# Attention fused with two feed-forward layers: for the tiles that hold the last 64 rows of two heads, the turned weights become the fixed operand of the product with the values, and the result is turned back

## The chip, the cores and the metric

The kernel runs on one core of a Trainium2 chip. The metric is device time in microseconds (us) of one launch, as the median of three runs. A core has a matrix engine (TensorE, PE in the profile; its weight loads are listed apart as PEld), a vector engine (DVE), a scalar engine (ACT), GpSimd (POOL), and SyncE (SP), which issues the DMAs here. Each engine takes its instructions in a fixed order and waits at an instruction until what it needs is there.

A matrix multiplication has a *fixed* operand (`lhsT`, loaded into the array first, up to 128 columns) and a *moving* operand (`rhs`, streamed through it column by column). An fp32 multiplication appears in the trace as two matmul records, each with a weight load of its own.

## The reference

```python
# q, k, v: (4 batches, 8 heads, 576 rows, 64)
scores = scale * np.matmul(q, k.transpose(0, 1, 3, 2))
kth = np.partition(scores, -32, axis=-1)[..., -32:-31]
scores = np.where(scores >= kth, scores, -1e9)
attn = softmax(scores)                              # over the last axis
attn_out = np.matmul(attn, v)
x = attn_out.transpose(0, 2, 1, 3).reshape(2304, 512)
x = leaky(x @ w_in1) @ w_out1                       # 512 -> 2048 -> 512
out = act2(x @ w_in2) @ w_out2                      # 512 -> 2048 -> 512
```

All of it is float32. `softmax`, `leaky` (the larger of h and 0.01 h) and `act2` (a parabola between -1 and 1) stand here for lines of the same meaning.

## The kernel before, in words

**Attention units.** A sequence of 576 rows is four tiles of 128 rows and a rest of 64. A unit of kind "m" is two tiles (256 rows) of one head. A unit of kind "r" is one tile of 128 rows made of the last 64 rows of head 2h and the last 64 rows of head 2h+1 (`st_scores`, L706 to L710). There are 64 units "m" and 16 units "r": twelve of these stand among the units of batch 2 and four among those of batch 3 (`REMS`, L32).

A unit goes through four steps. `scores` multiplies queries and keys on PE, and ACT copies the two halves (288 columns) to `s`. `topk` finds the 32nd largest score per row with MAX8 and MATCH_REPLACE on DVE (L570, L574), and ACT, POOL and DVE make the normalized weights `e` (L583 to L611). `pt_bank` turns `e` (128 rows x 576) into blocks of 116 keys x 128 rows on PE (L624; the last block has 112 keys) and ACT copies them to `ptr`. `pv` (L634) multiplies them with the values.

**`pv` of a unit "r" before.** The fixed operand is a block of values, `vl`: 116 keys x 128 columns, the 64 columns of one head twice. The moving operand is the 64 columns of `ptr` that belong to that head. So for each of the two heads there are five multiplications (one for each block of keys) of 64 moving columns, and the result has the value index on the partitions and the rows on the columns, as the next stage wants it. `gather` then copies 64x64 of it for each head to `xr` (L739, recorded at L361). Values of the first two batches take the same fp32 path for units "m", with 256 moving columns.

**Feed-forward layers.** Rows of 256 (one "m" pair of tiles for all heads) or 512 go through two layers. `hidden` (L804) and `sums` (L842) put fp32r multiplications on PE, three for each product (L766 to L768, and L837 to L839 for the second layer's sums). The groups are listed in `FLOW`; the last group, rows (3,0), (3,1) and "r", can start only when the last units are out, and "r" is the row block that all 16 units "r" fill.

**What sets the order.** All work is recorded as operations with an engine, an estimated duration, a priority and dependences (`Plan.op`). `Plan.run` (L130) plays this through in time and takes, on each engine, the ready operation of lowest priority number; the order that results is the program. Attention has the number of its unit (0 to 79), feed-forward products 10000 and more, so they fill what attention leaves free on PE. For a unit "r" before, each of the ten products is recorded with 112 ns (L657). From unit 20 on attention has two PSUM banks (6 and 7) for all its products (L335).

Of the kernel before, what the change touches and what calls it, by code (L numbers as in the profile page):

```python
# [23 lines left out]
NEG = -3.0e38  # L24
STEEP = 1.0e33
KB = 116
BUFS = dict(x=2, xraw=2, kk=5, vl=4, vv=4, kraw=3, px=8, vraw=2, qraw=3, qh=2, s=6, wk=3, e=4, m8=3, nb=3, sums=2, rc=2,
            pt=3, ptr=3, xb=2, t=3, gr=2, gt=3, wraw=2, wa=2, wb=2)
PREP = (0.7, 4.5, 0.05, 14, 14.0, 0.25)
HOP = 180  # L30
# [223 lines left out]
def t_a(n, psum=False):  # L254
    return 0.82 * n + (50 if psum else 95)
# [10 lines left out]
def t_m(n):  # L266
    return n / 2.4 + 14
# [7 lines left out]
def kernel(  # L275
# [4 lines left out]
    km: bass.AP,  # L280
    vm: bass.AP,
    vd: bass.AP,
    w_in1: bass.AP,
    w_out1: bass.AP,
    w_in2: bass.AP,
# [4 lines left out]
    nc = tc.nc  # L290
    B, H, D2, S = km.shape
    D = D2 // 2
# [3 lines left out]
    T = 256  # L296
    XW = 512
    QM = S // 128 * 128
    REM = S - QM
    HALF = S // 2  # L300
    NJ = vm.shape[3]
    cols = [slice(j * KB, min(S, (j + 1) * KB)) for j in range(NJ)]
    rows_of = [c.stop - c.start for c in cols]
    scale = 1.0 / float(D) ** 0.5
# [76 lines left out]
    def pe(fn, ns, w, r, prio, also=()):  # L381
        P.op("PE", ns, fn, w=w, r=r, prio=prio, also=also)
# [6 lines left out]
    idt = fixed([128, 128], F32, "idt")  # L389
# [98 lines left out]
    def lean_of(b, h):  # L488

        return b * H + h < NLEAN  # L490

    def plain_of(b, h):

        return b * H + h < NPLAIN
# [24 lines left out]
    def v_whole(b, h, pr):  # L519

        vt = new("vl", [128, NJ, 2 * D])
        dma(vt, lambda: vd[b, h], 320, [vt], [], pr + 0.5)
        return vt

    def q_new(src, n, pr, plain=False):
        raw = new("qraw", [128, QM])
        dma(lambda: raw()[:, 0:n], src, n / 2, [raw], [], pr)
        if plain:
            return raw
        qh = new("qh", [128, 2, QM], F32R)  # L530
        split(lambda a: qh()[:, a, 0:n], lambda: raw()[:, 0:n], n, qh, [raw], 0, pr)
        return qh
# [81 lines left out]
    def pt_bank(es, js, lean, pr):  # L614

        ps = bank(pr)
        p = rows_of[js[0]]
        blocks = [(e, j) for j in js for e in es]
        n = 128 * len(blocks)
        raw = new("ptr", [128, 512])  # L620

        def tr():
            for i, (e, j) in enumerate(blocks):
                nc.tensor.transpose(ps()[0:p, i * 128:(i + 1) * 128], e()[:, cols[j]], idt())  # L624

        pe(tr, 109 * len(blocks), [ps], list(es) + [idt], pr, [raw])
        act(lambda: raw()[0:p, 0:n], lambda: ps()[0:p, 0:n], t_a(n, True), [raw], [ps], pr)
        if lean:
            return raw
        pt = new("pt", [128, 2, 512], F32R)  # L630
        split(lambda a: pt()[0:p, a, 0:n], lambda: raw()[0:p, 0:n], n, pt, [raw], 0, pr)
        return pt

    def pv(es, jobs, lean, pr):  # L634

        w = 128 * len(es)
        per = 512 // w
        todo = [list(range(j, min(j + per, NJ - 1))) for j in range(0, NJ - 1, per)] + [[NJ - 1]]
        banks = [(pt_bank(es, js, lean, pr), js) for js in todo]
        out_ps = bank(pr)  # L640
        for bi, (pt, js) in enumerate(banks):
            for part in range(1 if lean else 2):
                def mm(bi=bi, pt=pt, js=js, part=part):
                    for (vt, c0, c1) in jobs:
                        for jj, j in enumerate(js):
                            p = rows_of[j]
                            c = slice(jj * w + c0, jj * w + c1)
                            nc.tensor.matmul(  # L648
                                out_ps()[:, c0:c1], lhsT=vt()[0:p, j, :],
                                rhs=pt()[0:p, c] if lean else pt()[0:p, part, c],  # L650
                                start=bi == 0 and part == 0 and jj == 0 and c0 == 0,
                                stop=bi == len(banks) - 1 and (lean or part == 1),
                                skip_group_check=True,
                            )

                n = jobs[0][2] - jobs[0][1]
                ns = max(4 * n / 2.4 if lean else t_m(n), 112)  # L657
                pe(mm, ns * len(js) * len(jobs), [out_ps], [pt if lean else (pt, (0, part))] + [vt for vt, _, _ in jobs], pr)
        return out_ps

    x_raw = {"r": fixed([128, KD, T], F32, "xr", lambda: pools["xr"])}

    def get_xraw(g):
        if g not in x_raw:
            x_raw[g] = new("xraw", [128, KD, T])
        return x_raw[g]
# [24 lines left out]
    def st_scores(u, pr):  # L691
        kind, b, a, h = u
        if kind == "m":
            plain = plain_of(b, h)
            if a == 0 or b not in JOINT:
                k_cur[b, h], v_cur[b, h] = k_new(b, h, pr, plain), v_new(b, h, pr)
            kk, vt = k_cur[b, h], v_cur[b, h]
            if b not in JOINT:
                q_cur["t"] = q_new(lambda: qm[b, h][:, a * T:(a + 1) * T], T, pr, plain)
            elif a == 0:  # L700
                q_cur["t"] = q_new(lambda: qm[b, h], QM, pr, plain)
            qh = q_cur["t"]
            t0 = 2 * a if b in JOINT else 0
            return dict(u=u, tiles=[scores([(qh, t0 + t, kk)], pr, plain) for t in range(2)], jobs=[(vt, 0, T)],
                        scale=scale / 2 if plain else scale)
        ks = [k_cur[b, 2 * h + e] if b == u_batch[0] else k_new(b, 2 * h + e, pr) for e in range(2)]  # L706
        vs = [v_whole(b, 2 * h + e, pr) for e in range(2)]
        qh = q_new(lambda: qp[b, h], T, pr)
        return dict(u=u, tiles=[scores([(qh, e, ks[e]) for e in range(2)], pr)], scale=scale,
                    jobs=[(vs[e], e * REM, (e + 1) * REM) for e in range(2)])  # L710

    def second():

# [6 lines left out]

    def st_out(s, pr):
        kind, b, a, h = s["u"]
        lean = kind == "r" or lean_of(b, h)
        ps = pv(s["es"], s["jobs"], lean, pr)
        if kind == "m":
            x = get_xraw((b, a))
            if h % 2 == 0 and not lean:
                xb_cur[a] = new("xb", [128, T])
            xb = xb_cur.get(a)
            c = h // 2  # L730
            gather(ps, (h % 2) * 64, 0, T, lambda: x()[:, c], (x, (c, h % 2)), xb, lean, pr)
            if h % 2 == 1 and not lean:
                P.op("P", t_p(T), lambda: nc.gpsimd.tensor_tensor(out=x()[:, c], in0=x()[:, c], in1=xb(), op=ALU.add),
                     w=[(x, (c, 0)), (x, (c, 1))], r=[xb], prio=pr)
        else:
            x = x_raw["r"]
            c = slice(b * REM, (b + 1) * REM)
            for e in range(2):
                gather(ps, e * 64, e * REM, (e + 1) * REM, lambda: x()[:, h, c], (x, (h, b, e)), None, True, pr)  # L739
# [205 lines left out]
def laid_out(inputs):  # L945

    x = {n: np.ascontiguousarray(inputs[n]) for n in _INS}
    q, k, v = x["q"], x["k"], x["v"]
    B, H, S, D = q.shape
    QM = S // 128 * 128  # L950
    REM = S - QM
    data = []

    def twice(a):
        a = a.transpose(0, 1, 3, 2)
        return np.concatenate([a, a], axis=2)

    data.append(("qm", twice(q[:, :, :QM])))
    qp = np.zeros((B, H // 2, 2 * D, 4 * REM), q.dtype)
    last = twice(q[:, :, QM:])  # L960
    for e in range(2):
        o = e * 128 + e * REM
        qp[..., o:o + REM] = last[:, e::2]
    data.append(("qp", qp))
    data.append(("km", twice(k)))
    nj = -(-S // KB)
    vp = np.zeros((B, H, nj * KB, D), v.dtype)
    vp[:, :, :S] = v
    vm = np.zeros((B, H, 128, nj, D), v.dtype)
    vm[:, :, :KB] = vp.reshape(B, H, nj, KB, D).transpose(0, 1, 3, 2, 4)  # L970
    data.append(("vm", vm))
    data.append(("vd", np.concatenate([vm, vm], axis=4)))
    for n in _INS[3:]:
        w = x[n]
        w = w.view(np.int64) if w.dtype == np.float64 else w
        if "_in" in n:
            kd, nf = w.shape[0] // 128, w.shape[1] // 128
            w = w.reshape(kd, 128, nf // 2, 2, 128).transpose(2, 1, 3, 0, 4)
        else:
            nf = w.shape[0] // 128  # L980
            w = w.reshape(nf // 2, 2, 128, w.shape[1]).transpose(0, 2, 1, 3)
        data.append((n, w.reshape(nf // 2, 128, -1)))
    data.append(("ident", np.eye(128, dtype=np.float32)))
    return [(n, np.ascontiguousarray(a)) for n, a in data]
# [18 lines left out]
```

## Time and profile before

| what | value |
|---|---|
| three runs | 1239.53, 1240.49, 1244.61 us; median 1240.49 us |
| profiled execution, its own time | 1239.65 us |
| its span, first to last instruction | 1237.9 us |
| PE busy | 1169.7 us (94%) |
| PEld busy | 996.9 us (81%) |
| DVE, ACT, POOL busy | 891.9, 854.3, 718.6 us |
| granted clock of TensorE, mean | 0.979 of full speed |
| moved by DMA | 238.58 MB, 193 GB/s |

Busy time of PE has modelled ends, since matmuls are pipelined: a record's duration is longer than the time until the next can start. What one record costs in a dense stretch is read from the distance between starts. The 16 units "r" multiply with the values between 495 and 938 us of the span; the page shows PE at nine tenths or more in nearly all 40 slices from the tenth on, while DVE, ACT and POOL fall off after some 930 us, when attention is over and the feed-forward layers of the last rows are left.

### The profile page before, as it was taken

To read this page: it belongs to the slowest core of one execution; us is meant where nothing else is said; L and a number is where in the kernel's file an instruction comes from. 1 tells how busy PE (TensorE), PEld (TensorE's weight loads), DVE (VectorE), ACT (ScalarE), POOL (GpSimd) and SP (SyncE) were. 2 spreads that over 40 slices of the span, in tenths; PEclk is the share of its full clock that TensorE was granted. 3 is DMA by queue.
4 is the path that set the end of the run, shared out by engine and by line. 5 is a ranking of instruction groups with operands and counts; after the bars stand their busy time and mean duration, and the time that the engine had idled before them with its cause. 6 is when DMAs were issued, how large, how long until landed. Compare 5 with 4: busy or idle time off the path is not lost.

```text
span 1237.9 us, 19284 instructions
## 1 busy us (share of the span) xinstructions
PE 1169.7 (94%) x6448; PEld 996.9 (81%) x6448; DVE 891.9 (72%) x1791; ACT 854.3 (69%) x1905; POOL 718.6 (58%) x820
## 2 busy tenths in 40 slices
PE   5678988887999999999999999999999999999998
PEld 4557878776878888888888888888888888888886
DVE  7999999999999999895999988979992000012221
ACT  6777999987888889897879788888643212142222
POOL 2434888764667669696878767778654222242221
PEclk8788999999999999999999999999999999999999
DMA  9744898986567555556566564443354423433333
GB/s 322 265 164 131 310 338 306 327 339 224 190 236 245 196 183 196 199 191 212 165 213 200 194 214 140 159 147 124 131 170 153 158 106 128 137 136 136 116 107 101
DMA packets 75444, 238.58 MB, mean 193 GB/s; under 512 B 8400, under 2 KB 14672, under 8 KB 71248
## 3 DMA queue, kind: packets, MB, share of 16 engines
q1 hardware_dynamic: 75344, 237.34, 55.3%
q8 instruction: 51, 0.84, 0.3%
q14 instruction: 49, 0.40, 0.1%
HBM read 199.03 MB, written 38.27 MB: 192 GB/s over the span
## 4 chain that ended last, share of the span: by engine, by line
PE 75%; ACT 10%; DVE 8%; POOL 4%; issue 2%; DMA 1%; SPq 0%; POOLq 0%; ACTq 0%; DVEq 0%
PE bank L766 14%; PE bank L768 14%; PE bank L767 14%; PE bank L648 10%; PE bank L624 5%; PE bank L547 5%; PE bank L837 5%; PE bank L839 5%; PE bank L838 5%; DVE m L570 3%; DVE wk L574 2%; ACT e L592 2%; DVE wb L456 2%; ACT s L361 1%; ACT e L363 1%
## 5 line engine op out<-in xcount | busy, mean ns | idle before, releaser
L377 POOL TENSOR_TENSOR gt<-gr,gt 128x512 fp32r<-128x512 f32 x144 | 191.6, 1332 | 253.9 <-ACT gt L361 132.2
L570 DVE MAX8 m<-wk 128x8 f32<-128x576 f32 x432 | 309.1, 747 | 0.8
L813 DVE TENSOR_SCALAR t<-bank 128x512 f32<-128x512 f32 x72 | 49.4, 687 | 241.5 <-PE bank L768 241.0
L574 DVE MATCH_REPLACE8 wk<-m,wk 128x576 f32<-128x576 f32 x288 | 212.3, 742 | 0.0
L766 PE MATMUL bank<-x,ring 128*128 128x512 f32 (+1 forms) x576 | 211.6, 367 | 0.2 <-DVE gr L816 0.2
L768 PE MATMUL bank<-x,ring 128*128 128x512 f32 (+1 forms) x576 | 205.8, 357 | 0.0
L767 PE MATMUL bank<-x,ring 128*128 128x512 f32 (+1 forms) x576 | 205.4, 357 | 0.0
L624 PE MATMUL bank<-idt,e 128*116 128x128 f32 (+1 forms) x720 | 114.4, 287 | 27.3 <-POOL e L609 22.1
L361 ACT COPY s<-bank 128x288 f32<-128x288 f32 x288 | 108.1, 404 | 35.4 <-PE bank L547 33.7
L624 PEld LDWEIGHTS bank<-idt,e 128*116 128x116 f32 (+1 forms) x720 | 87.8, 141 | 51.0 <-POOL e L609 29.8
L648 PE MATMUL bank<-ptr,vl 116*128 116x256 f32 (+3 forms) x640 | 124.8, 348 | 3.8 <-ACT ptr L361 3.6
L570 DVE MAX8 m<-s 128x8 f32<-128x576 f32 x144 | 103.9, 746 | 31.2 <-ACT s L361 31.2
L361 ACT COPY ptr<-bank 116x512 f32<-116x512 f32 (+1 forms) x224 | 107.6, 511 | 25.6 <-PE bank L624 24.3
L768 PEld LDWEIGHTS bank<-x,ring 128*128 128x128 f32 x576 | 108.4, 188 | 17.4
L377 POOL TENSOR_TENSOR pt<-ptr,pt 116x512 fp32r<-116x512 f32 (+1 forms) x96 | 106.3, 1130 | 25.1 <-ACT pt L361 23.5
L609 POOL TENSOR_SCALAR e<-e,rc 128x576 f32<-128x576 f32 x144 | 108.3, 762 | 20.3 <-DVE rc L607 17.5
L648 PEld LDWEIGHTS bank<-ptr,vl 116*128 116x128 f32 (+1 forms) x640 | 104.0, 204 | 19.0 <-ACT ptr L361 7.6
L766 PEld LDWEIGHTS bank<-x,ring 128*128 128x128 f32 x576 | 108.9, 189 | 11.7 <-DVE gr L816 0.7
L767 PEld LDWEIGHTS bank<-x,ring 128*128 128x128 f32 x576 | 108.9, 189 | 11.5 <-POOL x L377 0.5
L363 ACT ACTIVATE t<-t,half 128x512 f32<-128x512 f32 x72 | 52.0, 723 | 92.8 <-DVE t L813 92.6
L766 PE MATMUL bank<-gt,ring 128*128 128x512 f32 (+1 forms) x320 | 114.7, 358 | 0.0
L547 PE MATMUL bank<-kk,qh 128*128 128x288 f32 x512 | 101.2, 305 | 14.2 <-ACT s L361 6.3
(85 smaller groups left out, 2797.1 us busy)
## 6 DMA issues: line engine op xcount, KB each, us to landing
ring<-scr SPq DMA_DIRECT2D x224, 512.0 KB, 3.6
scr<-px SPq DMA_DIRECT2D x64, 512.0 KB, 4.2
vl<-in_vd_dram SPq DMA_DIRECT2D x56, 320.0 KB, 3.8
wraw<-in_moe_w_in_dram SPq DMA_DIRECT2D x16, 1024.0 KB, 6.0
wraw<-in_moe_w_out_dram SPq DMA_DIRECT2D x16, 1024.0 KB, 7.4
kraw<-in_km_dram SPq DMA_DIRECT2D x56, 288.0 KB, 4.2
qraw<-in_qm_dram SPq DMA_DIRECT2D x24, 256.0 KB, 4.0
out_dram<-t SPq DMA_DIRECT2D x16, 256.0 KB, 3.4
```

The lines of the kernel that those rows point to most:

```text
L361: nc.scalar.copy(out=out_(), in_=in_())
L363: nc.scalar.activation(out=out_(), in_=in_(), func=func, **a)
L377: lambda: nc.gpsimd.tensor_tensor(out=out_(), in0=in0(), in1=in1(), op=ALU.subtract),
L547: nc.tensor.matmul(ps()[:, 0:HALF], lhsT=qh()[:, at] if plain else qh()[:, part, at], rhs=kk()[:, c * HALF:(c + 1) * HALF], start=(i == 0) ...
L570: vec(lambda i=i, c=c, src=src: nc.vector.max(out=m()[:, i, c], in_=src()), 664, [(m, (i, r))], [src], pr)
L574: vec(lambda i=i, c=c, src=src, w=ws[i]: nc.vector.match_replace(out=w(), in_to_replace=m()[:, i, c], in_values=src(), imm_value=NEG), 720 ...
L609: P.op("P", T_NORM, lambda i=i: nc.gpsimd.tensor_scalar(out=es[i](), in0=es[i](), scalar1=rc()[:, i:i + 1], scalar2=1.0, op0=ALU.mult, op1 ...
L624: nc.tensor.transpose(ps()[0:p, i * 128:(i + 1) * 128], e()[:, cols[j]], idt())
L648: nc.tensor.matmul(out_ps()[:, c0:c1], lhsT=vt()[0:p, j, :], rhs=pt()[0:p, c] if lean else pt()[0:p, part, c], start=bi == 0 and part == 0 ...
L766: nc.tensor.matmul(ps, lhsT=wh, rhs=xh, start=first, stop=False, skip_group_check=True)
L767: nc.tensor.matmul(ps, lhsT=wh, rhs=xl, start=False, stop=False, skip_group_check=True)
L768: nc.tensor.matmul(ps, lhsT=wl, rhs=xh, start=False, stop=last, skip_group_check=True)
```

## The change

For units "r" `pv` is replaced by `pv_pair`. The turned weights `ptr` (116 keys x 128 rows) are the fixed operand, and the moving operand is a block of both heads' values side by side, 116 keys x 128 columns, from a new input `vp`. Five multiplications give 128 rows x 128 value columns. ACT copies that to a new buffer `y` (one buffer, 128x128), PE turns it with the identity into the same PSUM bank, and the same two 64x64 copies to `xr` follow. One DMA of 320 KB loads `vp` where two of 320 KB loaded `vd` twice. The multiplications are recorded with 218 ns each and the turn with 109 ns. For units "m" `pv` is written more simply and does what it did.

```diff
+    def v_pair(b, h, pr):
+
+        vt = new("vl", [128, NJ, 2 * D])
+        dma(vt, lambda: vp[b, h], 320, [vt], [], pr + 0.5)
+        return vt
...
+    def pv_pair(e, vt, pr):
+
+
+        banks = pt_banks([e], True, pr)
+        ps = bank(pr)
+        y = new("y", [128, 2 * D])
+        for bi, (pt, js) in enumerate(banks):
+            def mm(bi=bi, pt=pt, js=js):
+                for jj, j in enumerate(js):
+                    p = rows_of[j]
+                    nc.tensor.matmul(
+                        ps()[:, 0:2 * D], lhsT=pt()[0:p, jj * 128:(jj + 1) * 128], rhs=vt()[0:p, j, :],
+                        start=bi == 0 and jj == 0, stop=bi == len(banks) - 1,
+                    )
+
+            pe(mm, 2 * 109 * len(js), [ps], [pt, vt], pr, [y] if bi == 0 else [])
+        act(y, lambda: ps()[:, 0:2 * D], t_a(2 * D, True), [y], [ps], pr)
+        pe(lambda: nc.tensor.transpose(ps()[:, 0:128], y(), idt()), 109, [ps], [y, idt], pr)
+        return ps
...
-        vs = [v_whole(b, 2 * h + e, pr) for e in range(2)]
+        vt = v_pair(b, h, pr)
         qh = q_new(lambda: qp[b, h], T, pr)
-        return dict(u=u, tiles=[scores([(qh, e, ks[e]) for e in range(2)], pr)], scale=scale,
-                    jobs=[(vs[e], e * REM, (e + 1) * REM) for e in range(2)])
+        return dict(u=u, tiles=[scores([(qh, e, ks[e]) for e in range(2)], pr)], scale=scale, v=vt)
...
         else:
+            ps = pv_pair(s["es"][0], s["v"], pr)
             x = x_raw["r"]
...
     data.append(("vd", np.concatenate([vm, vm], axis=4)))
+    data.append(("vp", np.concatenate([vm[:, ::2], vm[:, 1::2]], axis=4)))
```

Two places show how the order moves. On PE, around the first unit "r" (batch 2, heads 0 and 1), the kernel before has these rows; L648 is `pv`, L624 turns the next unit's weights, L766 to L768 are feed-forward products:

```order
L648 MATMUL bank6_219<-ptr0_296,vl0_150 128x64 x4
L648 MATMUL bank6_219<-ptr0_296,vl1_158 128x64 x4
L648 MATMUL bank6_219<-ptr1_301,vl0_150 128x64
L648 MATMUL bank6_219<-ptr1_301,vl1_158 128x64
L766 MATMUL bank4_211<-x1_2345,ring4_493 128x512
L767 MATMUL bank4_211<-x1_2345,ring4_493 128x512
L768 MATMUL bank4_211<-x1_2345,ring4_493 128x512
L624 MATMUL bank7_225<-idt_146,e1_244 116x128 x4
```

In the changed kernel the same place reads so; L677 is the product in `pv_pair`, L684 the turn back, L631 and L792 to L794 are the former L624 and L766 to L768:

```order
L677 MATMUL bank6_222<-vl0_153,ptr0_299 128x128 x4
L677 MATMUL bank6_222<-vl0_153,ptr1_304 128x128
L792 MATMUL bank4_214<-x1_2348,ring4_496 128x512
L793 MATMUL bank4_214<-x1_2348,ring4_496 128x512
L794 MATMUL bank4_214<-x1_2348,ring4_496 128x512
L631 MATMUL bank7_228<-idt_149,e1_247 116x128 x4
L792 MATMUL bank4_214<-x1_2348,ring4_496 128x512
L793 MATMUL bank4_214<-x1_2348,ring4_496 128x512
L794 MATMUL bank4_214<-x1_2348,ring4_496 128x512
L684 MATMUL bank6_222<-idt_149,y0_4660 128x128
```

Ten products became five, and the turn stands behind six feed-forward products and four turns of the next unit's weights. On ACT, at the same unit, the kernel before has:

```order
L361 COPY xb_4367<-bank_225 64x256
L592 ACTIVATE e_322,sums_248<-e_322,nb_391 128x576
L361 COPY xr<-bank_219 64x64 x2
L583 ACTIVATE nb_234<-m_175 128x2x2
L363 ACTIVATE e_335<-s_227,nb_234 128x576
L361 COPY ptr_308<-bank_225 116x512
```

In the changed kernel ACT has, where L362, L364, L590 and L599 are the former L361, L363, L583 and L592:

```order
L362 COPY xb_4370<-bank_228 64x256
L599 ACTIVATE e_325,sums_251<-e_325,nb_394 128x576
L362 COPY y_4660<-bank_222 128x128
L590 ACTIVATE nb_237<-m_178 128x2x2
L364 ACTIVATE e_338<-s_230,nb_237 128x576
L362 COPY ptr_311<-bank_228 116x512
L362 COPY xr<-bank_222 64x64 x2
```

The copy to `y` takes the place of the copies to `xr`, which come three instructions later.

## Rows read from the trace of the kernel before

**Rows 1.** The page: busy us, share of the span, instructions of each engine.

```profile
PE 1169.7 (94%) x6448; PEld 996.9 (81%) x6448; DVE 891.9 (72%) x1791; ACT 854.3 (69%) x1905; POOL 718.6 (58%) x820
```

**Rows 2.** Busy time by stretch: us, engines busy (x instructions), clock, DMA share, GB/s.

```profile
495.00:938.00 443.00, 440.81 (x2508) 378.24 (x2507) 382.38 (x794) 353.52 (x840) 321.73 (x386) 1.00 0.52 174
938.00:969.00 31.00, 31.00 (x138) 25.24 (x137) 5.53 (x8) 10.57 (x20) 8.94 (x9) 1.00 0.58 194
969.00:1238.00 269.00, 263.15 (x1419) 225.82 (x1417) 33.13 (x48) 67.93 (x119) 69.51 (x60) 1.00 0.34 121
```

**Rows 3.** Groups by form: xcount | busy us, mean ns | idle before <-releasers.

```profile
L592 ACT ACTIVATE e<-e,nb 128x576 f32<-128x576 f32 x130 | 101.6, 783 | 2.6 <-POOL nb L585 2.3
...
L648 PE MATMUL bank<-ptr,vl 116*128 116x64 f32 x256 | 30.4, 272 | 0.0
...
L592 ACT ACTIVATION_READ_ACCUMULATOR e<-e,nb 128x1 f32 x130 | 25.7, 198 | 0.0
...
L648 PE MATMUL bank<-ptr,vl 112*128 112x64 f32 x64 | 9.8, 275 | 0.0
...
L361 ACT COPY xr<-bank 64x64 f32<-64x64 f32 x32 | 6.6, 207 | 26.5 <-PE bank L648 26.3
```

**Rows 4.** PE in order of time, a unit "r": start us, us, instruction.

```profile
503.59 2.34 PE L648 MATMUL bank<-ptr,vl 116*128 116x64 f32 x20
505.74 0.51 PE L547 MATMUL bank<-kk,qh 128*128 128x288 f32 x2
506.08 0.39 PE L766 MATMUL bank<-gt,ring 128*128 128x512 f32 x1
506.31 0.39 PE L767 MATMUL bank<-gt,ring 128*128 128x512 f32 x1
```

**Rows 5.** PE in order of time, a unit "m" of batch 1: 256 moving columns.

```profile
397.76 2.43 PE L648 MATMUL bank<-ptr,vl 116*128 116x256 f32 x10
399.84 0.59 PE L837 MATMUL bank<-px,gt 128*128 128x512 f32 x1
400.27 0.40 PE L838 MATMUL bank<-px,gt 128*128 128x512 f32 x1
```

**Rows 6.** PE from 926 us on: turns, the last unit "r", the last group's start.

```profile
926.13 1.03 PE L624 MATMUL bank<-idt,e 128*116 128x128 f32 x8
926.92 0.48 PE L766 MATMUL bank<-x,ring 128*128 128x512 f32 x1
927.24 0.39 PE L767 MATMUL bank<-x,ring 128*128 128x512 f32 x1
...
936.02 2.34 PE L648 MATMUL bank<-ptr,vl 116*128 116x64 f32 x20
938.17 0.48 PE L766 MATMUL bank<-x,ring 128*128 128x512 f32 x1
...
969.43 0.28 PE L766 MATMUL bank<-x,ring 128*128 128x256 f32 x1
```

**Rows 7.** All engines, 633 to 650 us: ACT's copies beside a unit "r".

```profile
636.82 2.34 PE L648 MATMUL bank<-ptr,vl 116*128 116x64 f32 x20
...
639.20 0.42 ACT L361 COPY xr<-bank 64x64 f32<-64x64 f32 x2 [1.96 <-PE bank L648]
...
645.54 0.26 ACT L361 COPY ptr<-bank 112x128 f32<-112x128 f32 x1
```

**Rows 8.** All engines, 300 to 306 us: PE held by a copy on ACT.

```profile
303.53 0.40 ACT L361 COPY s<-bank 128x288 f32<-128x288 f32 x1
...
303.99 0.53 PE L547 MATMUL bank<-kk,qh 128*128 128x288 f32 x2 [0.78 <-ACT s L361]
```

**Rows 9.** Line L648 (`pv`): what its engine sat idle for: us, times.

```profile
  ACT ptr L361: 11.4, 20
```

**Rows 10.** Waits from 560 to 620 us: us, times, longest.

```profile
DVE m L570 <- ACT s L361: 14.8, 3, 13.1
```

More of the change, by code (lines that the diff above doesn't have):

```diff
@@ L26 @@
 KB = 116
-BUFS = dict(x=2, xraw=2, kk=5, vl=4, vv=4, kraw=3, px=8, vraw=2, qraw=3, qh=2, s=6, wk=3, e=4, m8=3, nb=3, sums=2, rc=2,
+BUFS = dict(x=2, xraw=2, kk=5, vl=4, vv=4, kraw=3, px=8, vraw=2, qraw=3, qh=2, s=6, wk=3, e=4, m8=3, nb=3, y=1, sums=2, rc=2,
             pt=3, ptr=3, xb=2, t=3, gr=2, gt=3, wraw=2, wa=2, wb=2)
@@ L282 @@
     vd: bass.AP,
+    vp: bass.AP,
     w_in1: bass.AP,
@@ L632, in pt_bank, with pt_banks, pv @@
         return pt
-    def pv(es, jobs, lean, pr):
+    def pt_banks(es, lean, pr):
+        per = 512 // (128 * len(es))
+        todo = [list(range(j, min(j + per, NJ - 1))) for j in range(0, NJ - 1, per)] + [[NJ - 1]]
+        return [(pt_bank(es, js, lean, pr), js) for js in todo]
+    def pv(es, vt, lean, pr):
         w = 128 * len(es)
-        per = 512 // w
-        todo = [list(range(j, min(j + per, NJ - 1))) for j in range(0, NJ - 1, per)] + [[NJ - 1]]
-        banks = [(pt_bank(es, js, lean, pr), js) for js in todo]
+        banks = pt_banks(es, lean, pr)
         out_ps = bank(pr)
@@ L643, in mm @@
                 def mm(bi=bi, pt=pt, js=js, part=part):
[L644 to L654, printed above, removed]
@@ L656, in pv @@
-                n = jobs[0][2] - jobs[0][1]
-                ns = max(4 * n / 2.4 if lean else t_m(n), 112)
-                pe(mm, ns * len(js) * len(jobs), [out_ps], [pt if lean else (pt, (0, part))] + [vt for vt, _, _ in jobs], pr)
-        return out_ps
+                    for jj, j in enumerate(js):
+                        p = rows_of[j]
+                        c = slice(jj * w, jj * w + w)
+                        nc.tensor.matmul(
+                            out_ps()[:, 0:w], lhsT=vt()[0:p, j, :],
+                            rhs=pt()[0:p, c] if lean else pt()[0:p, part, c],
+                            start=bi == 0 and part == 0 and jj == 0,
+                            stop=bi == len(banks) - 1 and (lean or part == 1),
+                        )
@@ new lines, in pv @@
+                pe(mm, (4 * w / 2.4 if lean else t_m(w)) * len(js), [out_ps], [pt if lean else (pt, (0, part)), vt], pr)
+        return out_ps
+    def pv_pair(e, vt, pr):
[4 more added lines that the diff above has]
+            def mm(bi=bi, pt=pt, js=js):
+                for jj, j in enumerate(js):
+                    p = rows_of[j]
+                    nc.tensor.matmul(
+                        ps()[:, 0:2 * D], lhsT=pt()[0:p, jj * 128:(jj + 1) * 128], rhs=vt()[0:p, j, :],
+                        start=bi == 0 and jj == 0, stop=bi == len(banks) - 1,
+                    )
+            pe(mm, 2 * 109 * len(js), [ps], [pt, vt], pr, [y] if bi == 0 else [])
+        act(y, lambda: ps()[:, 0:2 * D], t_a(2 * D, True), [y], [ps], pr)
+        pe(lambda: nc.tensor.transpose(ps()[:, 0:128], y(), idt()), 109, [ps], [y, idt], pr)
+        return ps
@@ L703, in st_scores @@
             t0 = 2 * a if b in JOINT else 0
-            return dict(u=u, tiles=[scores([(qh, t0 + t, kk)], pr, plain) for t in range(2)], jobs=[(vt, 0, T)],
+            return dict(u=u, tiles=[scores([(qh, t0 + t, kk)], pr, plain) for t in range(2)], v=vt,
                         scale=scale / 2 if plain else scale)
         ks = [k_cur[b, 2 * h + e] if b == u_batch[0] else k_new(b, 2 * h + e, pr) for e in range(2)]
-        vs = [v_whole(b, 2 * h + e, pr) for e in range(2)]
+        vt = v_pair(b, h, pr)
         qh = q_new(lambda: qp[b, h], T, pr)
-        return dict(u=u, tiles=[scores([(qh, e, ks[e]) for e in range(2)], pr)], scale=scale,
-                    jobs=[(vs[e], e * REM, (e + 1) * REM) for e in range(2)])
+        return dict(u=u, tiles=[scores([(qh, e, ks[e]) for e in range(2)], pr)], scale=scale, v=vt)
     def second():
@@ L722, in st_out @@
         kind, b, a, h = s["u"]
-        lean = kind == "r" or lean_of(b, h)
-        ps = pv(s["es"], s["jobs"], lean, pr)
+        lean = lean_of(b, h)
         if kind == "m":
+            ps = pv(s["es"], s["v"], lean, pr)
             x = get_xraw((b, a))
```

## The prediction

> **What bounds the kernel now.** I read the page first. It gives PE 94% of the span [rows 1]. The reader is to see that no other engine comes near. Then I cut the span into stretches around the change [rows 2]. Between 495 and 938 us, where the 16 units "r" meet the values, PE is busy for 440.81 of 443 us at full clock, so it is idle for 2.2 us in all. DVE is the next, with 382.38 us (86%), then ACT with 353.52 us (80%). From 938 to 969 us PE is busy without a break, and after that for 263.15 of 269 us. So from 495 us on the time is the sum of what stands on PE, as long as its operands are there in time. Last I read the distances between starts on PE, since a record's own duration overlaps the next one's.
>
> **What goes.** Each unit "r" has ten products, twenty records; the groups by form count 256 + 64 = 320 records, which is 16 x 20 [rows 3]. The unit at 503.59 us runs undisturbed: its twenty records start there and the next product at 505.74 us, 2.15 us later [rows 4]. That product's two records take 0.34 us until 506.08, where the same pair of 288 columns takes about 0.26 us behind other work (the usual 0.23 us of a 512-column record times 288/512, twice), so about 0.08 us still belongs to the unit. I take 2.23 us for a unit, 112 ns a record, and 16 x 2.23 = 35.7 us in all. The last unit shows the same: 2.15 us to 938.17 [rows 6]. The planner had recorded 1.12 us for it.
>
> **What comes on PE.** Five products of 128 moving columns, ten records a unit. The trace has no such record, so I bound it. A record of 64 moving columns takes 112 ns. One of 256 takes 228 ns: ten of them from 397.76 to 399.84, and 0.20 us more that the next record is late (0.43 us to its successor, where such a record has 0.23 [rows 4]) [rows 5]. A record of 128 can't be shorter than that of 64, so 112 ns is the lower end. On the straight line between the two, as if loading and streaming stood one behind the other, it would be 112 + 116/3 = 151 ns; that is the upper end. The nearest row is the turn of weights, a record with 116 fixed and 128 moving columns: eight of them take 0.79 us, and the product behind them is late by 0.09 us (0.32 in place of 0.23), so 110 ns each [rows 6]. That 64 columns cost the same 112 ns as 128 moving columns in the turn says that something other than streaming sets the 112 ns, and I take it to be the load of the fixed operand, which is as wide as before. I take 112 ns: ten records are 1.12 us a unit.
>
> The turn back is one record with 128 fixed and 128 moving columns: 110 ns by the same row. So a unit gives back 2.23 - 1.12 - 0.11 = 1.00 us, and sixteen give 16.0 us. At the upper end of 151 ns it would be 2.23 - 1.51 - 0.11 = 0.61 us a unit, 9.8 us.
>
> [...]
>
> **What comes on ACT, and the new wait on PE.** The copy to `y` is 128x128 from PSUM; a copy of 112x128 takes 0.26 us [rows 7]. Sixteen are 4.2 us on an engine that has 89 us free in this stretch. Moreover ACT has stood idle for 26.3 us in all before the `xr` copies, as PE was later with the unit than ACT's order assumed [rows 3], for example 1.96 us at 639.20 [rows 7]. Most of that goes, so ACT gets time back.
>
> The turn waits for this copy, and behind it PE's queue stands still, feed-forward products included. The chain is: end of the last product, 0.04 us until ACT starts (639.16 to 639.20 [rows 7]), 0.26 us copy, and 0.06 us from the end of a copy (303.93) to PE's start (303.99) [rows 8], in sum 0.36 us. The pipe's drain of about 0.2 us comes before it (a record's 0.39 us against 0.23 between starts [rows 4]), so 0.56 us behind the last product's slot. In the changed order at least three feed-forward products stand between the two wherever I looked, 0.69 us, so the wait is covered if ACT is free. It isn't always: an activation of 783 ns and its read of 198 ns stand just ahead of the copy in several units [rows 3]. The row that prices this is the one of `pv`'s wait for `ptr`, the same kind of round trip, made some 220 times: 11.4 us in 20 waits over the whole run [rows 9], and hardly any of it in a stretch where PE idles 2.2 us in all. I take 0.1 us a unit, 1.6 us, between 0 and the slower rival's price below.
>
> **What is at nothing.** The loads: sixteen DMAs of 320 KB are gone, 5 MB of 239, in a stretch where the DMAs have a share of 0.52 [rows 2] and no product waits for `vl`. The single buffer `y` holds back the next unit's first product until the turn is done; there the order has feed-forward work in between. On PE nothing stands otherwise ahead of the first unit "r".
>
> **What is late next.** When PE is faster by 16 us, the weights `e` must be ready earlier. In the changed order 2601 feed-forward products stand ahead of the last unit's product with the values, where 2577 did; 24 x 0.23 = 5.5 us of the gain goes to them at once, and top-k has to be 10.5 us earlier by the last unit. DVE has 60.6 us free in the stretch, and part of that is a wait for scores (14.8 us between 560 and 620 [rows 10]), which come from PE and get earlier too. Behind attention there is cover: from 938.17 to 969.43 PE has 31 us of other rows' work before the first product of the rows "r" [rows 6]; counted in the order it is 108 products in place of 133, still some 25 us. So PE doesn't run dry there.
>
> **Sum.** 1239.65 us of the profiled execution, less 16.0, plus 1.6, is 1225.3 us. The median lies 0.84 us above the profiled execution, so I forecast 1226 us. Without waits and with the lower price it is 1224.5. A newly laid plan can shift some waits on its own; PE's idle time after 495 us is so small that this can hardly win, and may lose a few us.
>
> **Rivals.**
> (a) *Load and stream in series.* Then a record costs 151 ns, the gain is 9.8 - 1.6 = 8.2 us, and the time 1232 us. For it: the trace has no fp32 record of 128 moving columns with other values than the identity. Against it: the turns at 110 ns. [...] The rows at 112 and 228 ns leave room for it, the row of the turns does not.
> (b) *DVE keeps the pace.* Top-k does not follow by the 10.5 us, PE waits at the turns of weights, and all of that is given back: 16.0 - 1.6 - 10.5 = 3.9 us, 1236.6 us; by half it is 1231 us. For it: DVE is busy for 86%, and PE gets `e` shortly before it uses it. Against it: DVE waits for ACT's scores in the same stretch [rows 10], and ACT gets most of 26.3 us back [rows 3].
> (c) *Slower: PE stands at the turn back.* If ACT has two activations with their reads ahead of the copy in each unit, 2 x (783 + 198) = 1.96 us, the turn comes 1.96 + 0.56 - 0.69 = 1.8 us late, 29 us in all: 1239.65 - 16.0 + 29 = 1253 us. It decides from 1.0 us a unit on (nothing gained), and from 1.4 us it is slower by more than 0.5%. For it: an activation stands directly ahead of the copy in several units. Against it: those instructions run while PE does the products, and PE has the same dependence on `ptr` at small cost [rows 9].
>
> **Chances.** Forecast 0.69, from 1220 to 1230 us; (a) 0.08; (b) 0.14, half of it within 0.5%; (c) 0.05 slower and 0.04 where it just eats the gain. About 0.5% (6.2 us) is what a measurement can tell from no change. Faster: 0.69 + 0.08 + 0.07 = 0.84; same 0.07 + 0.04 = 0.11; slower 0.05. The range from 1220 to 1235 us takes in the forecast, (a), and (b) by half.
>
> **What would show it.** Right: 160 records of 128 columns at about 112 ns between starts, ten in 1.1 us; 16 turns at 110 ns; PE idle under 5 us between 495 and the end of attention, and that end near 928 us; ACT's wait before `xr` falls from 26.3 us to a few. Wrong: ten records in 1.5 us (a); long PE waits for POOL's `e` at the turns of weights (b); PE idle in front of the turn back, released by the copy to `y` (c).

## The result and the profile after

The changed kernel takes 1223.12 us (median of four runs, 1220.21 to 1226.7) where the kernel before takes 1240.01 us beside it. The ratio is 0.9859, with an interval from 0.9821 to 0.9896. Two later comparisons of the same two kernels are on record with 0.9871 each, from 0.9851 to 0.9891; by their medians they are 1221.57 beside 1239.31 us and 1224.67 beside 1240.26 us. The forecast was 1226 us, between 1220 and 1235 us.

The profiled execution took 1220.21 us, with a span of 1218.4 us. The page's first part answers to [rows 1]; the columns are the same:

```profile
PE 1151.4 (94%) x6304; PEld 978.9 (80%) x6304; DVE 893.7 (73%) x1791; ACT 857.7 (70%) x1921; POOL 719.1 (59%) x820
```

PE has 144 records and 18.3 us of busy time less, and the same share of a shorter span; DVE, ACT and POOL are within 3.4 us of what they were. To see where the time went, both spans are cut at the first and at the last product of a unit "r" with its values (before, the first stands at 492.95 us, so the stretch of [rows 2] begins 2 us behind it). Busy time by stretch, the kernel before:

```profile
0.00:492.95 492.95, 432.67 (x2371) 365.58 (x2372) 468.82 (x938) 420.50 (x924) 316.56 (x365) 0.95 0.70 249
492.95:938.10 445.15, 442.96 (x2528) 380.39 (x2526) 384.39 (x798) 355.31 (x843) 323.62 (x387) 1.00 0.52 174
938.10:1237.90 299.80, 294.05 (x1554) 250.96 (x1553) 38.66 (x56) 78.50 (x138) 78.45 (x68) 1.00 0.37 128
```

and the changed kernel:

```profile
0.00:490.47 490.47, 429.49 (x2372) 364.03 (x2372) 469.32 (x938) 420.39 (x924) 316.56 (x365) 0.95 0.70 250
490.47:924.98 434.51, 433.35 (x2407) 368.40 (x2406) 387.10 (x800) 359.84 (x860) 325.41 (x388) 1.00 0.50 169
924.98:1218.40 293.42, 288.56 (x1531) 246.48 (x1529) 37.27 (x54) 77.51 (x137) 77.15 (x67) 1.00 0.37 128
```

The first stretch, where the order on PE is the same, is 2.5 us shorter. That is scatter: in the repeats of the changed kernel it lasted 491.98 and 493.22 us. From the first unit "r" to the end it is 744.95 us before and 727.93 us after, 17.0 us less (727.32 and 727.38 us in the repeats). Of these, 10.6 us fall between the first and the last unit, and 6.4 us behind them. Most of the latter is work that moved: PE has 5.5 us less to do there, as more feed-forward products now stand ahead of the last unit. PE's busy time from the first unit on falls from 737.01 to 721.91 us, by 15.1 us, and its idle time from 7.9 to 6.0 us.

Most of that idle time is no wait of PE at all. It lies behind PE's last record, where only the last copies and stores are left. The last records, before and after:

```profile
1232.00 0.39 PE L839 MATMUL bank<-ring,gt 128*128 128x512 f32 x1
```

```profile
1213.40 0.39 PE L865 MATMUL bank<-ring,gt 128*128 128x512 f32 x1
```

From their ends to the end of the span it is 5.5 us before and 4.6 us after. Up to its last record PE is idle for 2.4 us before and 1.4 us after.

A unit "r" on PE and ACT in order of time, start us, us, instruction; it answers to [rows 4, 7] (rows are left out at the marks):

```profile
490.47 1.28 PE L677 MATMUL bank<-vl,ptr 116*128 116x128 f32 x10
491.50 0.47 PE L792 MATMUL bank<-x,ring 128*128 128x512 f32 x1
491.82 0.39 PE L793 MATMUL bank<-x,ring 128*128 128x512 f32 x1
491.92 0.78 ACT L599 ACTIVATE e<-e,nb 128x576 f32<-128x576 f32 x1
...
492.60 0.18 ACT L599 ACTIVATION_READ_ACCUMULATOR e<-e,nb 128x1 f32 x1
...
492.70 0.24 ACT L362 COPY y<-bank 128x128 f32<-128x128 f32 x1
492.95 0.40 PE L793 MATMUL bank<-x,ring 128*128 128x512 f32 x1
493.19 0.39 PE L794 MATMUL bank<-x,ring 128*128 128x512 f32 x1
493.42 0.27 PE L684 MATMUL bank<-idt,y 128*128 128x128 f32 x1
493.45 0.48 PE L792 MATMUL bank<-x,ring 128*128 128x512 f32 x1
493.77 0.40 PE L793 MATMUL bank<-x,ring 128*128 128x512 f32 x1
```

The reader is to see three things. Ten records take 1.03 us until the next start, and that one's successor is 0.09 us late, so a unit costs 1.12 us where it cost 2.23. Thirteen of the sixteen units have their ten records in one piece: ten of these take 1.03 to 1.12 us until the next start, and three take 1.13 to 1.23 us. The turn back (L684) costs 0.03 us until the next start and again 0.09 us behind it, 0.12 us. And although an exponential and its read of 0.96 us in all stand ahead of the copy to `y`, the copy is done at 492.94, half a microsecond before PE comes to the turn: the six feed-forward products and four turns in between cover it.

The groups by form, which answer to [rows 3] (xcount | busy us, mean ns | idle before, releaser):

```profile
L677 PE MATMUL bank<-vl,ptr 116*128 116x128 f32 x128 | 17.0, 275 | 0.0
...
L362 ACT COPY xr<-bank 64x64 f32<-64x64 f32 x32 | 6.6, 206 | 2.7 <-PE bank L684 2.3
...
L362 ACT COPY y<-bank 128x128 f32<-128x128 f32 x16 | 4.2, 265 | 7.8 <-PE bank L677 7.8
```

Where ACT stood 26.3 us before `xr`, it now stands 2.3 us before `xr` and 7.8 us before `y`. The lines of PE's idle time before the turn (L684) have one wait in all:

```profile
L684 PE MATMUL bank<-idt,y x16: 270/272/275, 493.4 to 925.8; 128*128 128x128 f32 x16
its engine sat idle before it (us, times) until:
  ACT y L362: 0.2, 1
```

### The profile page after: what moved, and what is told of

The parts are those of the page before. It is cut to its first block, busy times and chain, and to the rows that moved or that the text cites. A ratio compares the mean times of both kernels' runs of the same rounds, so it can differ in the third digit from the quotient of the medians.

```text
span 1218.4 us, 18965 instructions
## 1 busy us (share of the span) xinstructions
PE 1151.4 (94%) x6304; PEld 978.9 (80%) x6304; DVE 893.7 (73%) x1791; ACT 857.7 (70%) x1921; POOL 719.1 (59%) x820
## 4 chain that ended last, share of the span: by engine, by line
PE 73%; DVE 11%; ACT 9%; POOL 3%; issue 2%; DMA 1%; SPq 0%; POOLq 0%; ACTq 0%; DVEq 0%
PE bank L792 14%; PE bank L794 14%; PE bank L793 14%; PE bank L657 6%; PE bank L554 5%; PE bank L631 5%; PE bank L863 5%; PE bank L865 5%; PE bank L864 5%; DVE m L577 4%; DVE wk L581 3%; DVE wb L457 3%; ACT e L599 2%; PE bank L677 1%; ACT e L364 1%
## 5 line engine op out<-in xcount | busy, mean ns | idle before, releaser
L792 PE MATMUL bank<-x,ring 128*128 128x512 f32 (+1 forms) x576 | 211.0, 366 | 0.5 <-DVE gr L842 0.5
L794 PE MATMUL bank<-x,ring 128*128 128x512 f32 (+1 forms) x576 | 205.4, 357 | 0.0
L631 PE MATMUL bank<-idt,e 128*116 128x128 f32 (+1 forms) x720 | 114.3, 287 | 29.0 <-POOL e L616 23.8
L631 PEld LDWEIGHTS bank<-idt,e 128*116 128x116 f32 (+1 forms) x720 | 87.7, 141 | 52.5 <-POOL e L616 31.7
L362 ACT COPY s<-bank 128x288 f32<-128x288 f32 x288 | 107.5, 404 | 30.9 <-PE bank L554 29.3
L362 ACT COPY ptr<-bank 116x512 f32<-116x512 f32 (+1 forms) x224 | 107.0, 508 | 29.9 <-PE bank L631 28.0
L794 PEld LDWEIGHTS bank<-x,ring 128*128 128x128 f32 x576 | 108.1, 188 | 17.6
L378 POOL TENSOR_TENSOR pt<-ptr,pt 116x512 fp32r<-116x512 f32 (+1 forms) x96 | 106.0, 1127 | 21.5 <-ACT pt L362 16.1
L792 PEld LDWEIGHTS bank<-x,ring 128*128 128x128 f32 x576 | 108.4, 188 | 12.6 <-DVE gr L842 1.2
L792 PE MATMUL bank<-gt,ring 128*128 128x512 f32 (+1 forms) x320 | 115.8, 362 | 0.0
L364 ACT ACTIVATE gt<-bank 128x512 fp32r<-128x512 f32 x72 | 43.2, 600 | 102.1 <-PE bank L794 101.8
L364 ACT ACTIVATE t<-t,half 128x512 f32<-128x512 f32 x72 | 52.0, 722 | 86.7 <-DVE t L839 86.5
L794 PE MATMUL bank<-gt,ring 128*128 128x512 f32 (+1 forms) x320 | 112.3, 351 | 0.0
```

The lines of the kernel that those rows point to most:

```text
L362: nc.scalar.copy(out=out_(), in_=in_())
L364: nc.scalar.activation(out=out_(), in_=in_(), func=func, **a)
L378: lambda: nc.gpsimd.tensor_tensor(out=out_(), in0=in0(), in1=in1(), op=ALU.subtract),
L792: nc.tensor.matmul(ps, lhsT=wh, rhs=xh, start=first, stop=False, skip_group_check=True)
L794: nc.tensor.matmul(ps, lhsT=wl, rhs=xh, start=False, stop=last, skip_group_check=True)
```

## The experiments

All are compared with the kernel before, run beside them. As the first 490 us scatter by some microseconds between executions, this table also gives, from each profiled execution, the stretch from the first product of a unit "r" with the values to the end, with PE's busy and idle time in it. The part of the idle time that lies behind PE's last record is called the tail; it is about 4.65 us in some kernels and 5.5 us in others.

The scatter goes with the granted clock of TensorE (a mean over the execution, as a share of full speed): in the 17 executions of the kernel before that were run beside the first repeat, the one with the lowest mean clock (0.973) took 1245.36 us and the two with the highest (0.984) took 1236.67 and 1237.84 us. A straight line through all executions on record that list a clock, with a level of its own for each kernel and one slope for all, gives 0.65 us more time for each 0.001 of clock less. The last column is an estimate from that line: the distance to the changed kernel at equal clock, uncertain by 0.7 to 1.4 us.

| kernel | median us | ratio (interval) | stretch us | PE busy | PE idle | of it tail | at equal clock |
|---|---|---|---|---|---|---|---|
| before | 1240.01 | 1 | 744.95 | 737.01 | 7.9 | 5.5 | +17.5 |
| changed, first repeat | 1221.57 | 0.9871 (0.9851 to 0.9891) | 727.32 | 721.39 | 5.9 | 4.7 | 0 |
| changed, second repeat | 1224.67 | 0.9871 (0.9851 to 0.9891) | 727.38 | 721.47 | 5.9 | 4.6 | 0 |
| values fixed, no turn | 1223.25 | 0.9868 (0.9855 to 0.9882) | 728.55 | 720.68 | 7.9 | 4.6 | +1.2 |
| before, planned with true cost | 1236.78 | 0.9984 (0.9969 to 0.9999) | 742.26 | 736.65 | 5.6 | 4.6 | +14.6 |
| 64 fixed columns | 1224.21 | 0.9887 (0.9871 to 0.9903) | 729.70 | 721.05 | 8.7 | 5.5 | +2.2 |
| products twice | 1238.6 | 0.9999 (0.9983 to 1.0014) | 744.69 | 739.69 | 5.0 | 4.7 | +18.0 |
| turn without cover | 1232.75 | 0.9949 (0.9932 to 0.9966) | 737.77 | 725.58 | 12.2 | 4.7 | +10.6 |
| 64 columns, head by head | 1228.03 | 0.9893 (0.9864 to 0.9923) | 728.96 | 720.64 | 8.3 | 5.5 | +2.2 |
| 64 columns, heads in turn | 1225.36 | 0.9882 (0.9858 to 0.9906) | 726.48 | 717.24 | 9.2 | 5.5 | +0.2 |
| heads in turn, true cost | 1218.49 | 0.9824 (0.9805 to 0.9842) | 725.94 | 717.66 | 8.3 | 5.6 | -3.2 |

**Does PE's work count in full? The products twice.**

```diff
             pe(mm, 2 * 109 * len(js), [ps], [pt, vt], pr, [y] if bi == 0 else [])
+        for bi, (pt, js) in enumerate(banks):
+            def again(bi=bi, pt=pt, js=js):
...
+            pe(again, 2 * 109 * len(js), [ps], [pt, vt], pr)
```

> The changed kernel with the ten records of each unit r done twice into the same bank (the second time from the start again, so the result is the same); the planner knows of them. PE gets 160 records more between 490 and 925 us. Theory (PE's work counts in full): 160 x 112 ns = 17.9 us more than the changed kernel, about 1241 us. Rival (attention is held by DVE there, and PE has room): 10 us more or less, under 1233 us.

The lines left out are those of `mm`, with `start` set again at the first block. A unit's two sets start 1.12 us apart, and the second ends as the first:

```profile
490.31 1.28 PE L677 MATMUL bank<-vl,ptr 116*128 116x128 f32 x10
491.43 1.28 PE L687 MATMUL bank<-vl,ptr 116*128 116x128 f32 x10
492.55 0.60 PE L631 MATMUL bank<-idt,e 128*116 128x128 f32 x4
```

The stretch grows by 744.69 - 727.4 = 17.3 us for 160 x 112 ns = 17.9 us of work, and the median stands 14 to 17 us above those of the changed kernel, 18.0 us at equal clock. So PE's work counts one for one within the scatter, and the rival (DVE holds attention, PE has room) falls.

**What sets the 112 ns? The fixed operand cut to 64 columns.** The kernel before, otherwise unchanged:

```diff
+                            half_ = slice(c0, c1) if c1 - c0 == REM else slice(0, 2 * D)
...
-                                out_ps()[:, c0:c1], lhsT=vt()[0:p, j, :],
+                                out_ps()[half_, c0:c1], lhsT=vt()[0:p, j, half_],
```

> The kernel before, with the fixed operand of a unit r's products cut from 128 columns (the 64 of one head twice) to 64 (once); each product writes only the 64 partitions that are read later. Number of products and moving columns stay (20 records a unit). Theory (loading the fixed operand sets the 112 ns): a record costs 55 to 70 ns, a unit 1.1 to 1.4 us, the time about 1225 us (1221 to 1230). Rival (an fp32 record has a floor of about 110 ns, whatever its operands): 110 ns a record, and 1240 us.

This kernel sets `start` at the first head's first product alone, and its result is not the reference's (relative error 0.215); the work is the same. PE in order of time:

```profile
495.78 1.08 PE L649 MATMUL bank<-ptr,vl 116*64 116x64 f32 x20
496.79 0.65 PE L624 MATMUL bank<-idt,e 128*116 128x128 f32 x4
497.20 0.47 PE L767 MATMUL bank<-gt,ring 128*128 128x512 f32 x1
```

The same twenty records of 64 moving columns take 1.01 us until the next start, where they took 2.15 [rows 4]: about half, for half the fixed columns. The floor of 110 ns for a record falls. In the kernel before, the 128 fixed columns set the price: 112 ns a record, where 64 fixed columns cost 56 ns with the same 64 moving ones. That it is their load, and not for instance the writing of 128 result partitions, which are halved with them, stays argued. Nor does the run show that a load of 64 columns takes 55 ns: a quarter of the 228 ns of 256 moving columns [rows 5] is 57 ns, an estimate for 64 of them alone, so the stream may set the price here.

The run settles a rival besides. It keeps twenty records a unit and both DMAs of 320 KB, and its time at equal clock lies 2.2 us from the changed kernel's and 15 us from the kernel's before. So neither the halved number of records nor the sixteen DMAs that are gone make the gain.

**Which operand is fixed? The values, without the turn.** The changed kernel with the operands exchanged, and `y` and the turn left out, since the result then stands as `xr` wants it:

```diff
-                        ps()[:, 0:2 * D], lhsT=pt()[0:p, jj * 128:(jj + 1) * 128], rhs=vt()[0:p, j, :],
+                        ps()[:, 0:2 * D], lhsT=vt()[0:p, j, :], rhs=pt()[0:p, jj * 128:(jj + 1) * 128],
...
-            pe(mm, 2 * 109 * len(js), [ps], [pt, vt], pr, [y] if bi == 0 else [])
-        act(y, lambda: ps()[:, 0:2 * D], t_a(2 * D, True), [y], [ps], pr)
-        pe(lambda: nc.tensor.transpose(ps()[:, 0:128], y(), idt()), 109, [ps], [y, idt], pr)
+            pe(mm, 2 * 109 * len(js), [ps], [pt, vt], pr)
```

> The changed kernel with the operands of the units r exchanged: both heads' values (128 columns) are the fixed operand, all 128 rows of the turned weights the moving one. The result then comes out as the next stage wants it, so the copy to y and the turn back are gone. Theory (every us of work on PE after 495 us counts, and a record with 128 fixed and 128 moving columns costs 112 ns whichever operand is which): ten records a unit at 112 ns, and 16 x 0.11 us = 1.8 us less than in the changed kernel, so about 1221 us, 17 to 20 us below the kernel before. Rival (it matters which operand is fixed): the records come out longer than 120 ns and the time is above 1225 us.

> The changed kernel once more, beside the others on the same chip. Theory: 15 to 18 us below the kernel before. Rival (the gain of the first comparison was partly scatter between runs): 8 us or less.

Ten records again take 1.03 us until the next start and 0.09 us behind it:

```profile
493.05 1.28 PE L675 MATMUL bank<-ptr,vl 116*128 116x128 f32 x10
494.08 0.48 PE L788 MATMUL bank<-x,ring 128*128 128x512 f32 x1
494.40 0.40 PE L789 MATMUL bank<-x,ring 128*128 128x512 f32 x1
```

So the price does not depend on which operand is fixed; five products of 128 moving columns in place of ten of 64 bring the gain either way, and the rival with 120 ns falls. But the 1.8 us of the turn do not show in the time: 1223.25 beside 1221.57 us, and 1.2 us above the changed kernel at equal clock. In the stretch PE is busy 0.7 us less and idle 2.0 us more than in the repeats. Two of its waits in that run are new in size (us in total, times, longest):

```profile
PE bank L554 <- ACT xb L362: 1.6, 1, 1.6
PE bank L788 <- DVE gr L838: 1.2, 2, 1.0
```

The expectation for this run missed: it stands 16.1 us below the kernel before (1223.25 to 1239.31) and not 17 to 20, and that the turn's time comes off is not shown. The repeat of the changed kernel beside it stands 17.7 us below, within its band.

**Is it the plan? The kernel before, planned with the measured cost.**

```diff
-                ns = max(4 * n / 2.4 if lean else t_m(n), 112)
+                ns = 223 if n == REM else 4 * n / 2.4 if lean else t_m(n)
```

> The kernel before, with one number changed: the planner records 223 ns (as measured) in place of 112 ns for each product of a unit r. PE does the same work, in an order laid out with the true cost. Theory (the gain of the change is work taken off PE): no gain, 1237 to 1243 us, though ACT's wait before xr falls from 26.3 us to under 10. Rival (the gain came from a plan that now fits, ACT no longer standing before xr): 1225 to 1233 us.

ACT's wait before `xr` falls by half:

```profile
L361 ACT COPY xr<-bank 64x64 f32<-64x64 f32 x32 | 6.6, 206 | 13.5 <-PE bank L648 13.2
```

The time is 0.9984 of before (0.9969 to 0.9999), just below the expected band, and the stretch is 2.7 us shorter, mostly by PE's idle time (5.6 in place of 7.9 us). Of these 2.3 us, 0.8 us lie in the tail, and 1.5 us are waits of PE ahead of its last record. So a plan that fits is worth 2 to 3 us and not the 17: the theory holds, and the wait did fall, though not under the 10 us that I expected.

**What hides the turn? The turn straight behind the products.**

```diff
-        act(y, lambda: ps()[:, 0:2 * D], t_a(2 * D, True), [y], [ps], pr)
-        pe(lambda: nc.tensor.transpose(ps()[:, 0:128], y(), idt()), 109, [ps], [y, idt], pr)
+        def turn():
+            nc.scalar.copy(out=y(), in_=ps()[:, 0:2 * D])
+            nc.tensor.transpose(ps()[:, 0:128], y(), idt())
+
+        pe(turn, 109, [ps, y], [idt], -20.0)
```

> The changed kernel with the turn back put straight behind the products of its unit on PE, so that no feed-forward product stands between; ACT's copy to y is issued at the same place. Theory (the round trip over ACT is hidden by the products that the plan puts in between): PE now stands 0.56 us to 1.5 us at each of the 16 turns, 9 to 24 us more than the changed kernel, 1232 to 1247 us. Rival (the round trip is short enough to cost nothing even uncovered): within 3 us of the changed kernel.

A unit, on PE and ACT:

```profile
495.41 1.30 PE L677 MATMUL bank<-vl,ptr 116*128 116x128 f32 x10
496.77 0.26 ACT L684 COPY y<-bank 128x128 f32<-128x128 f32 x1
497.08 0.14 PEld L685 LDWEIGHTS bank<-idt,y 128*128 128x128 f32 x1 [0.56 <-ACT y L684]
497.09 0.33 PE L685 MATMUL bank<-idt,y 128*128 128x128 f32 x1 [0.37 <-ACT y L684]
```

Without cover the weight load of the turn is held 0.56 us in this unit. The waits of PE between 495 and 930 us name it 15 times:

```profile
PE bank L685 <- ACT y L684: 6.0, 15, 0.7
```

The stretch is 10.4 us longer than in the repeats (737.77 to 727.35), 0.65 us a unit: 6.3 us as idle time and 4.2 us as busy time. Of the latter most is the end of the last product, which no neighbour overlaps now (ten records are busy for 1.30 us, where they took 1.12 us in the full queue). This is the price of the slower rival's mechanism, at the lower end of what was expected, and it shows that the products in between hide it in the changed kernel.

**A step further: 64 fixed columns with one load of values.** Each head's 64 columns of `vp` alone are the fixed operand, its own 64 rows the moving one, without `y` and turn; the planner has 224 ns for a block of keys. The first kernel takes one head after the other and has the first of the two `for` lines, the second takes both in turn and has the second; the other lines are the same:

```diff
+                for (jj, j), z in [(x, z) for z in range(2) for x in enumerate(js)]:
+                for (jj, j), z in [(x, z) for x in enumerate(js) for z in range(2)]:
...
+                    c = slice(z * D, (z + 1) * D)
+                    nc.tensor.matmul(
+                        ps()[c, c], lhsT=vt()[0:p, j, c], rhs=pt()[0:p, jj * 128 + z * D:jj * 128 + (z + 1) * D],
```

> Each head's values alone as the fixed operand (64 columns), its own 64 rows as the moving one, each head writing its own 64 partitions, all products of the first head and then all of the second in a bank; one DMA of 320 KB as in the changed kernel, and no copy to y and no turn back. Theory (loading the fixed operand sets the price): 20 records at about 55 ns, 1.1 us a unit as in the changed kernel, without its turn: 1219 to 1225 us. Rival (the floor of 110 ns for a record): 2.2 us a unit and 1240 us.

> The same products with the two heads in turn: for each block of keys first the one head, then the other, so that neighbouring records use different columns of the array. Theory (loads of different columns still stand one behind the other): 55 ns a record, 1.1 us a unit, no difference from the run with one head after the other. Rival (records on different columns of the array run side by side): about 28 ns a record, 0.55 us a unit, 16 x 0.55 = 9 us less, about 1213 us.

Head by head, twenty records take 1.01 us until the next start and 0.11 us behind it (0.34 us where it is usually 0.23), as in the run with 64 fixed columns in the kernel before:

```profile
498.34 1.08 PE L676 MATMUL bank<-ptr,vl 116*64 116x64 f32 x20
499.35 0.50 PE L789 MATMUL bank<-x,ring 128*128 128x512 f32 x1
499.69 0.39 PE L790 MATMUL bank<-x,ring 128*128 128x512 f32 x1
```

In turn, they take 0.73 us and 0.11 us:

```profile
495.02 0.80 PE L676 MATMUL bank<-ptr,vl 116*64 116x64 f32 x20
495.75 0.50 PE L789 MATMUL bank<-x,ring 128*128 128x512 f32 x1
496.09 0.39 PE L790 MATMUL bank<-x,ring 128*128 128x512 f32 x1
```

The median of the first, 1228.03 us, lies above its band; its profiled execution reached the first unit "r" only after 498.34 us, which its edit does not touch, and its stretch (728.96 us) is like that of the run with the values fixed. Four of its six executions had a mean clock of 0.973 or 0.974 and took 1228.02 to 1229.43 us; the one at 0.983 took 1222.58 us. In turn, records come 42 ns apart and not 56 or 28, as if neighbours on different columns ran side by side in part. Neither theory had that. By the starts PE should save 16 x (1.12 + 0.12 - 0.84) = 6.4 us; its busy time falls by 4.2 us against the repeats, and where the rest is stays open. Idle time grows by 3.3 us, 0.9 us of it in the tail, so the time shows no difference.

**The same with the true cost in the plan.** 168 ns for a block of keys (four records of 42 ns) in place of 224:

> The run with the two heads in turn, planned with 168 ns for a block of keys (its four records as measured, 42 ns each) in place of 224 ns. Twenty records took 0.82 us a unit there, so PE has 16 x (1.13 + 0.11 - 0.82) = 6.7 us less to do than in the changed kernel. Theory (the time is PE's sum): 1214 to 1219 us, below the changed kernel. Rival (what PE gains here comes back as waits elsewhere, as in the run with both heads' values fixed): 1220 to 1226 us, no difference.

> The changed kernel beside the run with the heads in turn, on the same chip, so that the two can be compared within one call: 1220 to 1224 us by all theories.

It takes 1218.49 us beside 1224.67 us of the changed kernel, 0.9824 (0.9805 to 0.9842) of before, and is the fastest kernel of the study. The changed kernel itself lies above the 1220 to 1224 us expected for it here: its four executions had mean clocks of 0.973 to 0.981, those of the other kernel 0.978 to 0.981. At equal clock the two are 3.2 us apart, so about half of the 6.2 us between the medians goes with the clock. The stretch is 725.94 us, 1.4 us less than that of the changed kernel; PE is busy 3.8 us less in it and idle 2.4 us more, 1.0 us of that in the tail. Of the 3.9 us between the two profiled executions the other 2.5 us lie ahead of the first unit "r" (490.76 against 493.22 us), where nothing was edited. So the theory's band was met, but the gain over the changed kernel is 1.4 us in the stretch and 3.2 us at equal clock, not 6, and part of what PE saves comes back as idle time, as the rival had it.

## Why the prediction was right

**What bounds the kernel.** PE's sum, from 495 us on. The run with the products twice shows it: 17.3 us for 17.9 us of added work.

**What goes: 2.23 us a unit.** Read from the distance between starts; the run with 64 fixed columns confirms that the width of the fixed operand sets it (twenty records take 1.01 us until the next start there, 2.15 us before). That the cause is its load was argued in the prediction and still is.

**What comes: 1.12 us a unit for the products, 0.11 us for the turn.** Measured 1.12 and 0.12 us. The upper bound of 1.51 us, load and stream in series, fell at once, and rival (a) with it. The 112 ns in the sum were the lower end of the range, chosen by the row of the turns; that choice was right. One record of the turn lasts 272 ns from its start to its own end, and the products around it lose 0.12 us to it. The ten records of 128 moving columns cost 112 ns each, the same as the twenty of 64 before.

**The new wait: 1.6 us lost. This term had the wrong sign.** PE waited 0.2 us for the turn in all, not 1.6, and PE's idle time in the stretch fell by 1.9 us, 1.0 us of it ahead of PE's last record and 0.8 us in the tail. The cover of at least 0.69 us was right, and the run without cover prices what it hides, 0.65 us a unit. The row behind the 1.6 us was also read too widely: of the 224 copies to `ptr`, 96 go on to `pt` over ACT and POOL, so products wait for 128 of them and not for some 220. I had let the plan's fit count for ACT only and expected it to lose a few us on PE if anything; the run with the true cost in the plan takes 1.5 us off PE's waits, so such a fit may be what took the 1.0 us off here, though no run separates it. That the tail came out shorter was not foreseen and is luck; why it has two lengths is open. PE's busy time fell by 15.1 us, a little less than the 16.0 us of the working. So 15.1 + 1.9 = 17.0 us came in place of 16.0 - 1.6 = 14.4. That is the distance between the medians too, 1223 in place of 1226 us; the profiled execution, 19.4 us below the one before, owes 2.5 us more to the first 490 us.

**Rival (b), DVE keeps the pace.** It fell: in the same stretch DVE is busy 387.10 of 434.51 us (89%, before 86%), and among PE's waits between 490 us and the end none is for POOL's `e`. These are all of its waits there:

```profile
PE bank L554 <- ACT xb L362: 0.7, 1, 0.7
PE bank L792 <- DVE gr L842: 0.5, 2, 0.2
```

**Rival (c), PE stands at the turn.** An activation and its read do stand ahead of the copy, as in the unit shown, but PE is at its filling products meanwhile.

**Behind attention.** The last unit came at 925 us (forecast near 928), and from its end to the first product of the rows "r" PE had 25.8 us of other work (forecast some 25), and it stood idle for 0.2 us in all between the last unit and its own last record, so it did not run dry:

```profile
925.01 0.48 PE L792 MATMUL bank<-x,ring 128*128 128x512 f32 x1
...
950.82 0.28 PE L792 MATMUL bank<-x,ring 128*128 128x256 f32 x1
```

## What to carry to other kernels

Where the matrix engine is never idle, count its records by the distance between starts, and ask for each shape whether the width of the fixed operand or that of the moving one sets it: here 64 moving columns behind 128 fixed ones cost the same 112 ns as 128, and 56 ns behind 64 fixed ones. A round trip over another engine cost next to nothing here, as the order put other products into it; its price, 0.65 us, showed only when they were taken away. A saving of a few microseconds of work (the turn's 1.8 us) did not show in the time of a newly laid plan, whose waits were 2 us longer. So look for it in the busy and idle time of the stretch, split off what lies behind the engine's last record, and compare medians at equal granted clock: 0.001 of it went with 0.65 us here.

## What the runs showed of the hardware that was not expected

Fp32 records of 64 fixed columns that write different halves of the partitions come closer together if they come in turn: twenty take 0.84 us in turn and 1.12 us one head after the other, 42 and 56 ns a record. Between 56 ns and its half, the 28 ns estimated for records side by side, this looks like a partial overlap; what limits it was not tested.
